# The third channel group of a causal convolution moved from TensorE to GpSimd, ahead of a fused feed-forward

## The chip, the cores and the metric

The kernel runs on one core of a Trainium2 chip. The metric is the device time of one execution in microseconds (us). The engines' names in the profile are PE (TensorE; PEld is its weight load), DVE (VectorE), ACT (ScalarE), POOL (GpSimd) and SP (SyncE, which here only issues DMAs).

## The reference, cut to what matters

```python
batch, seq, d_model = 8, 3904, 192      # x: (8, 3904, 192) float32
n_heads, kernel_size, d_ff = 8, 7, 1024

def _attn_ref(x, weight):               # a causal convolution of 7 taps along seq
    w = softmax(weight, axis=-1)        # (heads, 7); a head is 24 channels
    x_pad = np.concatenate([np.zeros((B, 6, D)), x], axis=1)
    x_unf = x_pad[:, idx, :].reshape(B, S, K, H, group)
    return np.einsum('hk,bskhg->bshg', w, x_unf).reshape(B, S, D)

def _moe_ref(x, w1, w2, w3, w_out):     # over 31232 tokens of 192 channels
    return ((x @ w1) * (x @ w2)) @ w3 @ w_out
```

## The kernel before, in words

The 31232 tokens are held as two strips of 15616 (NS = 2, strip r), which are worked on side by side. The 192 channels are held as three groups of 64; in each of the tiles xT[0], xT[1] and xT[2] the partitions are 64 channels of strip 0 and the same 64 of strip 1, and the columns are tokens. These tiles are rings of 2048 tokens, four rounds of 512 (CH).

The product w3 @ w_out is formed once at the start. Then each of 31 rounds R of 512 tokens has two steps. `first_product(R)` (L385 to L394) multiplies xT[0], xT[1], xT[2] by w1 and w2 in that order of k, accumulating in PSUM; ScalarE copies one result to SBUF (asb, L392), VectorE multiplies it with the other (abT, L394). `second_product(R, r)` (L410, L415, L418) multiplies abT by the joined weights, ScalarE copies the result out (osb), and SP issues the DMA to the output.

The convolution is itself a matmul. Windows of 32 tokens (26 new ones and 6 from before) lie on 32 partitions, loaded by GpSimd's queue with a cast to bf16 (`load_x`, tile xb, L117); a 32x32 band matrix of one head's taps (Aband) gives 26 convolved tokens. TensorE does 16 such small matmuls per head piece (`conv`, L282) into the PSUM tile cps; VectorE and ScalarE cast it into convo (L290). `store` (L315, L321) writes convo to the DRAM tensor rows from SP's queue, 26 rows a window, and `transposes(R)` (L355) brings 512 rows of each of the three groups back as xT, by a transposing DMA on SP's queue.

Windows come in blocks: SIZES gives 11 blocks of 20 to 80 windows. A unit is one call of conv for some heads of a block. From block 4 on there are 26 units.

The order of the steady part is written out by hand. Its phases p = 0 to 14 have the first products of two rounds each (none in phase 0, rounds 2p+1 and 2p+2 after it), then the second products of the two rounds before. Between second products stand convolution units: after the first and the third of four, and in phases 0 and 1 after the second too. The last unit of a block is followed by that block's stores. At a phase's end the transposes of two rounds are issued as far as stored rows allow. Loads of xb for later blocks are issued behind a small copy (pace, L563), with which GpSimd waits for the phase's first round. Where a window begins a sequence, GpSimd sets six rows of xb to zero (L558) once the load has landed.

All engines run their queues in order. A wait on SP holds every later DMA on SP; a wait on GpSimd holds its later loads and copies.

Of the kernel before, what the change touches and what calls it, by code (L numbers as in the profile page):

```python
# [8 lines left out]
FP32 = mybir.dt.float32  # L9
BF16 = mybir.dt.bfloat16  # L10
# [6 lines left out]
def kernel(  # L17
# [10 lines left out]
    nc = tc.nc  # L28
# [26 lines left out]
    MAXN = 20  # L55
    HW = 6

    def tok(i):
# [16 lines left out]
        return stage.tile(shape, dtype, tag="slot", bufs=5, name=name)  # L75

    rows = dram.tile([TS, NP * NS * Q], BF16, name="rows")
    x_rows = x.rearrange("b s d -> (b s) d")


    def shape_of(b):
        n = SIZES[b] // 4
        m = n // (1 if b < 3 else 2)
        return n, m, n // m

    def parts_of(b):
        return [range(4)] if 4 * shape_of(b)[1] <= MAXN else [range(2), range(2, 4)]

    xb_of, zero_rows = {}, {}

# [15 lines left out]
    def load_x(b, parts=(0, 1)):  # L106
        tiles = xb_of.setdefault(b, {})
        zeros_of = zero_rows.setdefault(b, [])
        n, m, E = shape_of(b)
        for js in [v for q, v in enumerate(parts_of(b)) if q in parts]:  # L110
            xb = work.tile([128, len(js) * m, D], BF16, tag="xb", bufs=6, name="xb")
            for j in js:
                tiles[j] = (xb, (j - js[0]) * m)
            for e in range(E):
                for s, t, w in runs_of(b, js, e):
                    for r in range(NS):
                        nc.gpsimd.dma_start(  # L117
                            out=xb[group(r, e), s:s + w, :],
                            in_=bass.AP(tensor=x.tensor, offset=(r * TS + t - PAD) * D,
                                        ap=[[D, C], [E * ST * D, w], [1, D]]))  # L120
                for j in js:
                    for u in range(m):
                        i, s = FIRST[b] + j * n + u * E + e, tiles[j][1] + u
                        if i % WB == 0 and i:
                            zeros_of += [(xb, group(r, e).start, s) for r in range(NS)]
                        if i == NWIN - 1:
                            nc.gpsimd.memset(xb[group(1, e), s, :], 0.0)
                            t = tok(i) - PAD
                            nc.gpsimd.dma_start(out=xb[group(0, e), s, :],
                                                in_=x_rows[t:t + C, :])  # L130
                            p = group(1, e).start
                            nc.gpsimd.dma_start(out=xb[p:p + PAD + LAST, s, :],
                                                in_=x_rows[TS + t:TS + t + PAD + LAST, :])


    taps = const.tile([H, K], FP32)
# [115 lines left out]

    xT = [const.tile([128, RING], BF16, name=f"xT{k}", tag=f"xT{k}") for k in range(NP)]

    convo_of, heads_left = {}, {}
    wt = {}

    def segments(c0, n):
# [4 lines left out]
            c0, n = c0 + m, n - m  # L263
        return out

    def conv(b, h0, nh, evict=(nc.scalar.copy,), es=None):
        n, m, E = shape_of(b)
        es = range(E) if es is None else es
        if b not in convo_of:
            convo_of[b] = work.tile([128, n, NP, NS, Q], BF16, tag="convo", bufs=2, name="convo")  # L270
            heads_left[b] = H * E
        convo = convo_of[b]
        wd = nh * G
        cps = {e: banks("cps") for e in es}
        for q in range(nh):
            cs = slice((h0 + q) * G, (h0 + q + 1) * G)
            for j in range(4):
                xb, s = xb_of[b][j]
                for e in es:
                    for r in range(NS):  # L280
                        o = cps[e][j * C:j * C + C, r, 0:m * wd]
                        nc.tensor.matmul(  # L282
                            o.rearrange("p (w g) -> p w g", g=wd)[:, :, q * G:(q + 1) * G],
                            Aband[group(r, e), h0 + q, :], xb[group(r, e), s:s + m, cs],
                            start=True, stop=True)
        for f, e in zip(evict, es):
            src = cps[e][:, :, 0:m * wd].rearrange("p r (w g) -> p r w g", g=wd)
            o = 0
            for k, c0, c in segments(h0 * G, wd):
                f(out=convo[:, e::E, k, :, c0:c0 + c]  # L290
                    .rearrange("p w r g -> p r w g"), in_=src[:, :, :, o:o + c])
                o += c
        heads_left[b] -= nh * len(es)
        if not heads_left[b]:
            del xb_of[b]

    stored, sent = [0], [3]
# [1 line left out]
    def store(b, first=0):  # L299
        stored[0] = tok(FIRST[b] + SIZES[b]) if b + 1 < NB else TS  # L300
        n = SIZES[b] // 4
        convo = convo_of[b]
        for j in range(4):
            w = 0
            while w < n:
                i = FIRST[b] + j * n + w
                if i < first:
                    w += 1
                    continue
                left = WB - 1 - i % WB  # L310
                src = convo[C * j:C * j + ST, w:w + max(1, min(n - w, left))]
                src = src.rearrange("s w k r g -> s w (k r g)")
                j0 = tok(i)
                if left == 0:
                    nc.sync.dma_start(out=rows[j0:j0 + LAST, :], in_=src[0:LAST, 0, :])  # L315
                    w += 1
                    continue
                m = min(n - w, left)
                dst = rows[j0:j0 + ST * m, :].rearrange("(w s) c -> s w c", s=ST)
                for s0, s1 in ((0, 16), (16, ST)):  # L320
                    nc.sync.dma_start(out=dst[s0:s1], in_=src[s0:s1])  # L321
                w += m
# [28 lines left out]
    def transposes(R, first=0):  # L351
        t0, t1 = max(R * CH, first), min((R + 1) * CH, TS)
        a = t0 % RING
        for k in range(NP):
            nc.sync.dma_start_transpose(  # L355
                out=xT[k][:, a:a + t1 - t0], in_=rows[t0:t1, k * 128:(k + 1) * 128])


    def w_of(i, k, r):
        if k == 2:  # L360
# [119 lines left out]

    conv(0, 0, 4, evict=(A,))
    swap_w(0, 0, 256, P)
    conv(0, 4, 4, evict=(V,))
    warm(2)
    first_transposes()
    for k in (2, 1):
# [29 lines left out]
    first_product(0, {  # L518
        0: seq((swap_w, 1, 256, HC, A, (1,))),
        2: later_loads,  # L520
        4: seq((conv, 1, 0, 4)),
        5: seq((conv, 1, 4, 4)),
        6: seq((pe_transposes, 1))})
    first_product(1, {
        2: seq((conv, 2, 0, 4)),
        3: seq((conv, 2, 4, 4), (w3_turn, 0)),
        4: seq((pe_transposes, 2), (store, 2, LAG_ROWS // ST))})
    first_product(2, {
        1: seq((w3_turn, 2)),
        3: seq((w3_product, 0), (w3_product, 2), (w3_turn, 4), (w3_turn, 6),  # L530
               (conv, 3, 0, 4, (A,), (0,)), (conv, 3, 0, 4, (V,), (1,))),
        4: seq((w3_product, 4), (w3_product, 6),
               (conv, 3, 4, 4, (A,), (0,)), (conv, 3, 4, 4, (V,), (1,)),
               (store, 3), (transposes, 3), (transposes, 4))})
    sent[0] = 5


    phases = [()] + [(R, R + 1) for R in range(LAG + 1, NR, 2)]
    assert phases[-1][-1] == NR - 1
    def heads_of(b):  # L540
        return max(n for n in (2, 4, 8) if n * shape_of(b)[1] * G <= CH)

    units = [(b, h, heads_of(b)) for b in range(4, NB) for h in range(0, H, heads_of(b))]
    loads = [(b, e) for b in range(6, NB) for e in range(len(parts_of(b)))]

    def convolve():
        if units:
            b, h, n = units.pop(0)
            conv(b, h, n, (V, A))
            if h + n == H:  # L550
                store(b)

    pace = const.tile([1, 2], BF16)
    done = 0
    for p, rounds in enumerate(phases):
        for b, h, n in units[:3]:
            for xb, p0, w in zero_rows.pop(b, []):
                nc.gpsimd.memset(xb[p0:p0 + PAD, w, :], 0.0)  # L558
        for j, R in enumerate(rounds):
            first_product(R)  # L560
            if loads and (j == 0 or p == 1):
                nb, part = loads.pop(0)
                P(out=pace, in_=abT_of[R][0:1, JT - 1, 1, 0:2])  # L563
                load_x(nb, (part,))
# [43 lines left out]
```

## Time and profile before

| | |
|---|---|
| median of 3 runs | 519.27 us (518.94 to 520.60) |
| profiled execution | 519.05 us, span 517.2 us |
| granted TensorE clock | 1.0 of full |
| busy: PE, DVE, ACT, POOL | 99%, 66%, 64%, 14% of the span |
| convolution matmuls L282 | 1216, 15.5 us busy |
| DMA | 64.81 MB, mean 125 GB/s |
| xb loads on GpSimd's queue (L117) | 74, 48.0 us busy |

Busy times are sums over instructions; matmuls overlap, and their ends are modelled, so a PE that reads 99% tells that it rarely waits, not that it is at its peak. The chain of waits leads from the last instruction back through what released each step. A timeline gives start, duration, engine, line and count of merged instructions, and in brackets the idle time ahead and who ended it.

### The profile page before, as it was taken

How to read it: one execution, taken by the hardware profiler on the slowest of the kernel's cores; microseconds unless marked ns; L12 is line 12 of the kernel's file. 1: busy time of each engine (PE TensorE's matmuls, PEld its weight loads, DVE VectorE, ACT ScalarE, POOL GpSimd, SP SyncE). 2: the span in 40 equal slices, each digit the busy share in tenths (PEclk: the TensorE clock that was granted, in tenths of full speed). 3: DMA queues.
4: the chain of work that ended last, by engine and by line, in shares of the span. 5: the costliest groups of instructions: out<-in, count | busy, mean ns of one | idle time of the engine just before them, and what ended most of it. 6: DMA issues, size and time to landing. Idle time of an engine off the chain costs nothing.

```text
span 517.2 us, 14447 instructions
## 1 busy us (share of the span) xinstructions
PE 511.6 (99%) x6271; PEld 333.4 (64%) x6272; DVE 343.5 (66%) x326; ACT 332.6 (64%) x376; POOL 73.3 (14%) x140
## 2 busy tenths in 40 slices
PE   8999999999999999999999999999999999999997
PEld 4446946758567585674856758567585575856777
DVE  7898478494783947839578395783946839377370
ACT  6886476674765757657576575765757657476562
POOL 9864004030020200402002020030000000000000
PEclk9999999999999999999999999999999999999999
DMA  9999779999666995669956696456725066240304
GB/s 146 150 185 176 143 187 158 223 120 186 118 77 151 149 152 119 77 142 155 151 123 77 147 166 120 123 61 143 146 84 123 1 147 137 64 107 2 123 1 153
DMA packets 137936, 64.81 MB, mean 125 GB/s; under 512 B 86805, under 2 KB 137873, under 8 KB 137873
## 3 DMA queue, kind: packets, MB, share of 16 engines
q1 hardware_dynamic: 92625, 45.92, 42.1%
q0 software_dynamic: 45232, 17.97, 31.5%
q8 instruction: 49, 0.80, 0.6%
q14 instruction: 14, 0.11, 0.1%
q10 hardware_dynamic: 16, 0.00, 0.0%
HBM read 36.22 MB, written 34.80 MB: 137 GB/s over the span
## 4 chain that ended last, share of the span: by engine, by line
PE 97%; DVE 1%; ACT 1%; issue 0%; DVEq 0%
PE ops L410 32%; PE pa L385 30%; PE pb L385 30%; PE cps L282 2%; PE wps L475 1%; PE warm L196 1%; ACT asb L392 1%; DVE abT L394 0%; ACT convo L290 0%; PE ops L428 0%; PE tps L345 0%; PE tps L330 0%; DVE xT L337 0%; DVE xb L238 0%; DVE Aband L248 0%
## 5 line engine op out<-in xcount | busy, mean ns | idle before, releaser
L394 DVE TENSOR_TENSOR abT<-asb,pb 128x1024 bf16<-128x1024 bf16 x240 | 292.7, 1220 | 81.5 <-ACT asb L392 65.7
L392 ACT CAST asb<-pa 128x1024 bf16<-128x1024 f32 x244 | 247.0, 1012 | 63.4 <-PE pa L385 63.1
L385 PE MATMUL pb<-xT,wn 64*128 64x512 bf16 (+1 forms) x744 | 198.4, 373 | 0.0
L385 PE MATMUL pa<-xT,wn 64*128 64x512 bf16 (+1 forms) x744 | 197.5, 373 | 0.2
L385 PE MATMUL pa<-xT,ws 64*128 64x512 bf16 (+1 forms) x744 | 197.5, 373 | 0.0
L385 PE MATMUL pb<-xT,ws 64*128 64x512 bf16 (+1 forms) x744 | 196.1, 373 | 0.0
L385 PEld LDWEIGHTS <-wn 64*128 64x128 bf16 x1488 | 138.1, 94 | 85.7 <-issue 2.2
L385 PEld LDWEIGHTS <-ws 64*128 64x128 bf16 x1488 | 131.5, 94 | 70.8 <-POOL ws L182 0.4
L410 PE MATMUL ops<-W_sb,abT 128*128 128x192 bf16 x1936 | 166.9, 246 | 0.0
L410 PEld LDWEIGHTS <-abT 128*128 128x128 bf16 x1936 | 157.6, 98 | 10.0 <-issue 9.4
L415 ACT COPY osb<-ops 128x768 f32<-128x768 f32 (+1 forms) x61 | 48.4, 793 | 108.8 <-PE ops L410 106.5
L290 DVE CAST convo<-cps 128x320 bf16<-128x320 f32 (+5 forms) x46 | 33.8, 766 | 75.4 <-PE cps L282 73.8
L117 POOL DMA_DIRECT2D xb<-in_x_dram x74 | 48.0, 656 | 7.3 <-PE pa L385 3.2
L563 POOL COPY pace<-abT 1x2 bf16<-1x2 bf16 x10 | 1.7, 174 | 245.1 <-DVE abT L394 245.1
L290 ACT CAST convo<-cps 128x640 bf16<-128x640 f32 (+5 forms) x54 | 32.5, 645 | 1.7 <-PE cps L282 1.6
L282 PE MATMUL cps<-xb,Aband 32*32 32x240 bf16 (+2 forms) x1216 | 15.5, 245 | 0.5 <-DVE Aband L248 0.4
L282 PEld LDWEIGHTS <-Aband 32*32 32x32 bf16 x1216 | 8.4, 88 | 7.1 <-issue 6.3
L432 DVE COPY osb<-ops 128x192 f32<-128x192 f32 x1 | 0.4, 357 | 11.7 <-PE ops L428 11.7
L456 POOL DMA_DIRECT2D w3b<-in_moe_w_dram x12 | 7.1, 598 | 4.0 <-DMA xb<-in_x_dram 3.1
L182 POOL COPY ws<-wn 64x256 bf16<-64x256 bf16 x17 | 6.7, 396 | 0.9
L196 PE MATMUL warm<-zeros 128*128 128x512 bf16 (+1 forms) x12 | 4.6, 518 | 1.4 <-DVE zeros L140 1.3
L475 PEld LDWEIGHTS <-w3T 128*128 128x128 bf16 x64 | 5.2, 98 | 1.0 <-issue 0.4
(57 smaller groups left out, 54.1 us busy)
## 6 DMA issues: line engine op xcount, KB each, us to landing
out_dram<-osb SPq DMA_DIRECT2D x60, 384.0 KB
xb<-in_x_dram POOLq DMA_DIRECT2D x40, 240.0 KB, 7.0
rows<-convo SPq DMA_DIRECT2D x17, 240.0 KB
rows<-convo SPq DMA_DIRECT2D x17, 150.0 KB
xb<-in_x_dram POOLq DMA_DIRECT2D x8, 192.0 KB, 4.4
rows<-convo SPq DMA_DIRECT2D x12, 120.0 KB
xT<-rows SPq DMA_TRANSPOSE x84
w3b<-in_moe_w_dram POOLq DMA_DIRECT2D x4, 256.0 KB, 5.0
```

What stands on the lines that cost most here:

```text
L117: nc.gpsimd.dma_start(out=xb[group(r, e), s:s + w, :], in_=bass.AP(tensor=x.tensor, offset=(r * TS + t - PAD) * D, ap=[[D, C], [E * ST * D ...
L182: f(out=wsw[k][Q * h:Q * h + Q, lo:hi], in_=wn[k][Q - Q * h:2 * Q - Q * h, lo:hi])
L196: nc.tensor.matmul(t[:, j % 2, 0:wd], zeros[:, 0:128], zeros[:, 0:wd], start=True, stop=True)
L282: nc.tensor.matmul(o.rearrange("p (w g) -> p w g", g=wd)[:, :, q * G:(q + 1) * G], Aband[group(r, e), h0 + q, :], xb[group(r, e), s:s + m, ...
L290: f(out=convo[:, e::E, k, :, c0:c0 + c] .rearrange("p w r g -> p r w g"), in_=src[:, :, :, o:o + c])
L385: nc.tensor.matmul(p[:, r, f * N:f * N + N], w_of(i, k, r)[rs, ft * 128:(ft + 1) * 128], xT[k][rs, r0:r0 + N], start=(k == 0), stop=(k == ...
L392: nc.scalar.copy(out=asb[:, :, 0:per * N], in_=pa[:, :, 0:per * N])
L394: nc.vector.tensor_tensor(out=ab[:, f0, :, 0:N], in0=asb[:, :, 0:N], in1=pb[:, :, 0:N], op=ALU.mult)
L410: nc.tensor.matmul(ops[:, g // 2, (g % 2) * D:(g % 2) * D + D], ab[:, jt, r, g * 128:(g + 1) * 128], W_sb[:, jt, :], start=(jt == 0), stop ...
L415: nc.scalar.copy(out=osb.rearrange("p (a g) d -> p a (g d)", g=2), in_=ops[:, 0:ng // 2, 0:2 * D])
L456: nc.gpsimd.dma_start(out=t[C * i:C * i + C], in_=bass.AP(tensor=moe_w3.tensor, offset=j0 * 128 * DFF + i * GQ, ap=[[DFF, C], [C * DFF, 4 ...
L475: nc.tensor.matmul(wps[:, q, 0:D], w3T[:, g, q, :, :, t].rearrange("p j b -> p (j b)"), wo_b[:, g, t, :], start=(g + t == 0), stop=(g == G ...
```

## The change

Three things change from block 4 (round 5) on.

TensorE convolves only channels 0 to 127. Blocks 4 to 11 have 64 windows (the last 56), and a unit is 64 channels of a block, so that there are 16 units; since heads are 24 channels wide, a unit has three or four pieces of heads. A table (places) says how many units a phase has. xb, convo, rows stores and the transposes of xT cover 128 channels.

Channels 128 to 191 go another way. A DMA on GpSimd's queue casts them from x to a DRAM tensor rows_c in bf16 (`cast_c`), 1024 tokens of both strips at a time (a chunk; 13 chunks). A transposing DMA on SP's queue, issued at the end of phase p after the last output and before the transposes of xT, brings chunk p as the tile raw, with 16 tokens from before it (`raw_transpose`). In phase p+1 GpSimd convolves it: for each tap a multiply of raw, shifted by the tap's distance, with a column of taps, and an add to acc, in float32; the tap of distance 0 comes last, in two halves, and writes xT[2] (`conv_c`). Where a sequence starts inside a chunk, each step is split in two. The products of phase p+2 read it.

The taps reach GpSimd as a tile wC, one row per partition, through a small DRAM tensor: GpSimd divides by the sum, and SP issues seven small DMAs (`load_taps`) before the stores of blocks 2 and 3.

On GpSimd's queue the order of a phase is: zero rows, the cast of chunk p, the convolution of chunk p-1, pace, loads of xb.

```diff
-    SIZES = [20, 20, 20, 40, 40] + [80] * 5 + [64]
+    SIZES = [20, 20, 20, 40] + [64] * 7 + [56]
+    SPLIT = 4
+    WC = 2 * Q
...
+    RC = FIRST[SPLIT] * ST // CH
...
+    def width_of(b):
+        return D if b < SPLIT else WC
...
-            xb = work.tile([128, len(js) * m, D], BF16, tag="xb", bufs=6, name="xb")
+            wd = width_of(b)
+            xb = work.tile([128, XN], BF16, tag="xb", bufs=6, name="xb")
+            xb = xb[:, 0:len(js) * m * wd].rearrange("p (w d) -> p w d", d=wd)
...
-    def conv(b, h0, nh, evict=(nc.scalar.copy,), es=None):
+    def conv(b, c0, wd, evict=(nc.scalar.copy,), es=None):
...
-        for q in range(nh):
-            cs = slice((h0 + q) * G, (h0 + q + 1) * G)
+        c = c0
+        while c < c0 + wd:
+            h = c // G
+            c1 = min(h * G + G, c0 + wd)
             for j in range(4):
...
-                            Aband[group(r, e), h0 + q, :], xb[group(r, e), s:s + m, cs],
+                            Aband[group(r, e), h, :], xb[group(r, e), s:s + m, c:c1],
...
-        for k in range(NP):
+        for k in range(NP if R < RC else WC // Q):
             nc.sync.dma_start_transpose(
                 out=xT[k][:, a:a + t1 - t0], in_=rows[t0:t1, k * 128:(k + 1) * 128])
...
+    def load_taps():
+        nc.sync.dma_start(out=taps_d, in_=taps)
+        for r in range(NS):
...
+                nc.sync.dma_start(out=wC[r * Q + c - WC:r * Q + c1 - WC, :],
+                                  in_=taps_d[h:h + 1, :].to_broadcast([c1 - c, K]))
...
+    def cast_c(i):
+        t0, t1 = chunks[i]
+        t0 = t0 if i else t0 - HALO
+        for r in range(NS):
+            nc.gpsimd.dma_start(out=rows_c[t0:t1, r * Q:r * Q + Q],
+                                in_=x_rows[r * TS + t0:r * TS + t1, WC:D])
+
+    def raw_transpose(i):
+        t0, t1 = chunks[i]
+        raw_of[i] = work.tile([128, HALO + 2 * CH], BF16, tag="raw", bufs=2, name="raw")
+        nc.sync.dma_start_transpose(out=raw_of[i][:, 0:HALO + t1 - t0],
+                                    in_=rows_c[t0 - HALO:t1, :])
+
+    def conv_c(i):
+        t0, t1 = chunks[i]
+        raw = raw_of.pop(i)
+        acc = work.tile([128, 2 * CH], FP32, tag="acc", bufs=1, name="acc")
+        part = work.tile([128, 2 * CH], FP32, tag="part", bufs=1, name="part")
+        starts = [z for z in range(0, TS, S) if t0 <= z < t1]
+
+        def times(out, lo, hi, d):
+            nc.gpsimd.tensor_scalar(out=out, in0=raw[:, HALO + lo - t0 - d:HALO + hi - t0 - d],
+                scalar1=wC[:, K - 1 - d:K - d], scalar2=None, op0=ALU.mult)
+
+        def add(out, lo, hi, d):
+            p = part[:, lo - t0:hi - t0]
+            times(p, lo, hi, d)
+            nc.gpsimd.tensor_tensor(out=out, in0=p, in1=acc[:, lo - t0:hi - t0], op=ALU.add)
+
+        times(acc[:, 0:t1 - t0], t0, t1, 1)
+        for z in starts:
+            nc.gpsimd.memset(acc[:, z - t0:z - t0 + 1], 0.0)
+        for d in range(2, K):
+            for lo, hi in zip([t0] + [z + d for z in starts], starts + [t1]):
+                add(acc[:, lo - t0:hi - t0], lo, hi, d)
+        for lo in range(t0, t1, CH):
+            hi = min(lo + CH, t1)
+            add(xT[2][:, lo % RING:lo % RING + hi - lo], lo, hi, 0)
...
-        for b in (4, 5):
-            load_x(b)
+        load_x(4)
+        nc.gpsimd.tensor_scalar(out=taps, in0=taps, scalar1=total, scalar2=None, op0=ALU.mult)
+        load_taps()
+        cast_c(0)
+        load_x(5)
...
-    units = [(b, h, heads_of(b)) for b in range(4, NB) for h in range(0, H, heads_of(b))]
+    units = [(b, c) for b in range(SPLIT, NB) for c in range(0, WC, Q)]
...
+    places = {0: 2, 1: 2, 2: 1, 3: 1, 4: 2, 5: 1, 6: 1, 7: 1, 8: 1, 9: 2, 10: 1, 11: 1}
...
+        if 0 < p < len(chunks):
+            cast_c(p)
+        if 0 < p <= len(chunks):
+            conv_c(p - 1)
         for j, R in enumerate(rounds):
             first_product(R)
-            if loads and (j == 0 or p == 1):
+            if loads and j == 0:
...
-            if n in (0, 2) or (n == 1 and p < 2):
+            if n in (0, 2)[:places.get(p, 0)]:
                 convolve()
+        if p < len(chunks):
+            raw_transpose(p)
```

More of the change, by code (lines that the diff above doesn't have):

```diff
@@ L288, in conv @@
             o = 0
[L289 to L290 removed]
+            for k, lo, c in segments(c0, wd):
+                f(out=convo[:, e::E, k, :, lo:lo + c]
                     .rearrange("p w r g -> p r w g"), in_=src[:, :, :, o:o + c])
                 o += c
[L293 to L294 removed]
+        left_of[b] -= wd * len(es)
+        if not left_of[b]:
             del xb_of[b]
@@ new lines @@
+    chunks = [(R * CH, min((R + 2) * CH, TS)) for R in range(RC, NR, 2)]
+    raw_of = {}
+    def cast_c(i):
[9 more added lines that the diff above has]
+                                    in_=rows_c[t0 - HALO:t1, :])
```

65 lines of the change are left out of this document (37 added, 28 removed).

## The prediction, made before the changed kernel was run

> **What bounds the kernel now.** I read the page first (busy times, chain), then the stretches of single phases, then the groups by shape, then the timelines of SyncE and GpSimd, because the new work is handed over through those two queues.
>
> ```profile
> PE 511.6 (99%) x6271; PEld 333.4 (64%) x6272; DVE 343.5 (66%) x326; ACT 332.6 (64%) x376; POOL 73.3 (14%) x140
> PE 97%; DVE 1%; ACT 1%; issue 0%; DVEq 0%
> ```
>
> TensorE carries 97% of the chain that ended last, while VectorE and ScalarE have a third of the span free. So only two things move the end: TensorE work removed, and TensorE waits added. The profiled execution took 519.05 us (span 517.2 us, 1.85 us around it); the median of the runs is 519.27 us, 0.04% away. I sum against 519.05. A measurement of this kernel can tell about 0.3%, 1.6 us, from no change.
>
> Four phases (two rounds of products each), as stretches: length, then busy time and instructions of PE, PEld, DVE, ACT, POOL, clock, DMA share, GB/s.
>
> ```profile
> 65.00:97.86 32.86, 32.86 (x418) 21.06 (x420) 23.13 (x21) 22.06 (x25) 5.70 (x10) 1.00 1.19 183
> 195.10:227.52 32.42, 32.42 (x387) 21.02 (x388) 21.91 (x19) 21.13 (x23) 5.50 (x11) 1.00 0.56 105
> 357.19:389.52 32.33, 32.33 (x386) 20.94 (x388) 21.51 (x19) 20.81 (x23) 0.00 (x0) 1.00 0.58 124
> 421.86:453.35 31.49, 31.49 (x322) 20.67 (x324) 19.53 (x16) 19.34 (x20) 0.00 (x0) 1.00 0.50 113
> ```
>
> They hold three, two, two (192 columns) and no convolution units. The differences are the whole price of convolution on TensorE: 32.42 - 31.49 = 0.93 us for two units of 32 matmuls of 240 columns, 0.84 us for two of 192 columns.
>
> Groups by shape:
>
> ```profile
> L282 PE MATMUL cps<-xb,Aband 32*32 32x240 bf16 x640 | 8.5, 266 | 0.0
> L282 PE MATMUL cps<-xb,Aband 32*32 32x120 bf16 x448 | 5.5, 216 | 0.5 <-DVE Aband L248 0.4
> L394 DVE TENSOR_TENSOR abT<-asb,pb 128x1024 bf16<-128x1024 bf16 x240 | 292.7, 1220 | 81.5 <-ACT asb L392 65.7
> L182 POOL COPY ws<-wn 64x256 bf16<-64x256 bf16 x17 | 6.7, 396 | 0.9
> L563 POOL COPY pace<-abT 1x2 bf16<-1x2 bf16 x10 | 1.7, 174 | 245.1 <-DVE abT L394 245.1
> ```
>
> **TensorE: what is removed.** From block 4 on, the kernel before issues 896 convolution matmuls (128 in block 4, 640 in blocks 5 to 9, 128 in block 10). The changed kernel has 8 blocks of 7 head pieces x 16 = 112, again 896: the cuts at channels 64 and 128 split heads, so a third fewer channels gives no fewer instructions (its instruction order shows as many PE rows as before). And the price goes by instruction, hardly by column: the chain shows 64 matmuls of 120 columns in 0.66 us (10.3 ns each), 32 of 240 in 0.35 (10.9). What falls is the 0.1 us that each unit costs in switching: 26 units become 16. Before, phase 0 pays 12.64 us for four output products that take 10.67 in a phase without units, so 1.97; phase 1 pays 1.37; eight phases 0.93; two 0.84: 12.5 us in all. After: a pair of units has 48 + 64 matmuls, 112 x 10.1 ns + 2 x 0.1 = 1.33, eight pairs 10.7. Saving **1.8 us**; bounds 1.0 (nothing per matmul, ten switches) and 4 (a third of the 12.5).
>
> ScalarE and VectorE lose a third of the evictions at L290 and DMA a third of the stores and xb bytes. Worth nothing here: they lie under TensorE, and if that cover went they would save under 1 us a phase.
>
> **GpSimd: what is added.** Per chunk of 1024 tokens: a multiply (d=1), five times multiply and add (d=2..6), and d=0 as two halves of 512. No row shows these forms on GpSimd. The nearest: a copy of 256 elements takes 396 ns and one of 2 elements 174, so 0.17 us fixed and 0.87 ns an element net, 1.55 gross. Low bound: an add costs what a copy does (1.06 us for 1024, chunk 15 us). High bound: gross rate, an add reading two operands in turn (3.2 us, chunk 34 us). I take 1.0 ns an element and operand, near the net rate because the instructions are long, a little above it because sums are float32: multiply 0.17 + 1.02 = 1.2, add 0.17 + 2.05 = 2.2. Chunk: 1.2 + 5 x 3.4 + 2 x (0.68 + 1.19) = 22.0; each instruction waits for the one before it, 0.07 us by diag's memset and select (1.03 to 1.10), x15 = 1.0. **23 us**, first half of xT[2] ready after 21. Three chunks that hold a sequence start split every step: +2.5.
>
> The Trainium skill's "GPSIMD Engine Reference", section 3, has 4497 ns for a float32 add of 2048; an estimate from it is 2.25 us for 1024, beside the 2.2 above. The same section keeps elementwise work on VectorE, which speaks against this change; by its add price with the copy rows for multiplies the chunk is 22 us.
>
> A phase is 32 us, so GpSimd's sum (23, casts 1.6, loads 2.7 to 5.4) fits. What must be asked is when a chunk may start and must end. The raw of phase p is convolved in phase p+1 for the products of phase p+2. It must end (first half) by the start of the next phase's products plus 0.45 us, as TensorE can do the k=0 and k=1 matmuls first. It may start when the raw transpose landed, and that stands on SP behind the out DMAs and, in some phases, the stores:
>
> ```profile
> 66.65 1.13 SPq L418 DMA_DIRECT2D out_dram<-osb  x2
> 67.89 6.06 SPq L321 DMA_DIRECT2D rows<-convo  x8
> ...
> 187.12 9.21 SPq L418 DMA_DIRECT2D out_dram<-osb  x4
> 196.43 8.04 SPq L355 DMA_TRANSPOSE xT<-rows  x6
> 219.54 6.11 SPq L418 DMA_DIRECT2D out_dram<-osb  x3
> 226.11 0.76 SPq L321 DMA_DIRECT2D rows<-convo  x2
> 226.96 0.25 SPq L315 DMA_DIRECT2D rows<-convo  x1
> 227.27 9.57 SPq L321 DMA_DIRECT2D rows<-convo  x8
> 236.94 1.42 SPq L418 DMA_DIRECT2D out_dram<-osb  x1
> 238.46 12.12 SPq L355 DMA_TRANSPOSE xT<-rows  x6
> ```
>
> Phases end at 195.10 and 227.52. Without stores SP reaches its transposes 1.3 us after the end; behind stores of an 80-window block 10.9 us after it. A 64-window block has 0.8 of that, so about 8. A transpose of 512 rows takes 1.2 us to issue, 1040 rows 2.4; landing is not shown, I take 2 (0 to 5). So raw lands at end + 5.7 in plain phases, + 8.4 where stores come in mid-phase (3, 6, 8, 11), + 12.4 where they come last (1, 4, 9). Phase 0: SP starts its outs at 66.65; three outs 1.7, stores of 64 windows 6.06 x 1.6 = 9.7, one out, transpose 2.4, landing: 82.
>
> - Chunk 0: 82 + 21.1 = 103.1; TensorE needs it at 97.85 + 0.45. **Wait 4.8 us.**
> - Plain phases: 5.7 + 21.1 = 26.8 of about 32.2: hidden, 5 us to spare. Mid-phase stores: 29.5, hidden.
> - Late stores (phases 4 and 9): 12.4 + 21.1 = 33.5 against 32.7: **0.8 us each**.
> - Phase 3: chunk 1 (a split one, raw late) ends late, then eight loads of 0.67, then the memset of zero rows waits for that load to land (5 us), and the cast and chunk 2 stand behind it on GpSimd. Carried through phase by phase: **2.6 us** at the start of phase 4.
>
> Sum of waits 9.0. **519.05 - 1.8 + 9.0 = 526.3 us.**
>
> ```profile
> 207.36 0.17 POOL L563 COPY pace<-abT 1x2 bf16<-1x2 bf16 x1 [29.19 <-DVE abT L394]
> 207.90 4.83 POOL L117 DMA_DIRECT2D xb<-in_x_dram  x8 [0.36 <-PE pa L385]
> ```
>
> These loads now come after the chunk, some 15 to 25 us later. They fill blocks used one or two phases on, and land in 7 us: I cost that at nothing; with the cover gone a load would cost the first unit up to 10 us, once. The tap loads stand on SP before the stores of block 3, which wait for their eviction until 49 us anyway: nothing, at most 1 us.
>
> VectorE's product L394 has one operand in PSUM and one in SBUF. The Trainium skill's "SBUF — State Buffer", section on the shared port rule, has GpSimd blocked only by VectorE instructions with two SBUF inputs or in a two-port mode; by that no contention, and no run here shows it.
>
> **Rivals.**
> 1. GpSimd hides everything (faster). If a chunk takes at most 17.5 us (an add at 1.4 us), even chunk 0 is ready in time: 519.05 - 1.8 = **517.2 us**. For it: 17.5 lies inside my bounds, and one-operand copies run at 0.87 ns. Against: an add reads two operands and float32.
> 2. Between 17.5 and 21 us only chunk 0 waits, by 0 to 3 us: **517.5 to 520**, no difference.
> 3. GpSimd becomes the bound. From 27 us on, late raws, loads and casts add up and most phases wait: at 1.2 ns an operand the same reckoning gives 31 us of waits, **548 us**; at the gross rate (34 us) some 91, **608 us**. For it: the gross rate is the only one that a row shows without subtraction.
> 4. The saving is absent: if units cost by matmul and the switch is not saved, 1.8 us are missing from each case. Within the ranges.
>
> After a wait TensorE may restart slowly: at the start, six warm matmuls of 512 columns take 2.74 us, about twice their later rate. The Trainium skill's "TensorE: Matmul & The Clock Gate", Part 1, has half clock after an idle window of about 3.4 us; one such restart would add an estimated 2 us, inside the range.
>
> **Numbers.** Forecast case (chunk 21 to 27 us, 520.6 to 545) 0.44; rival 1 0.18; rival 2 0.11; rival 3 0.27. Faster 0.18, same 0.11, slower 0.71. The range from 517 (rival 1) to 549 (rival 3's first price) leaves out about 0.2, nearly all above.
>
> **What would show it.** Right: POOL groups near 1.2 (multiply) and 2.2 us (add); the longest TensorE gap, near 5 us, before the round-5 products at about 98 us, released by POOL's add into xT; smaller ones at the starts of phases 4, 6, 11; phases without waits 0.2 us shorter than before. Wrong: no PE wait on POOL (rival 1), waits at every phase (rival 3), PE phases shorter by over 0.4 us (convolution priced by column), waits on xb loads or on rows transposes, or L394 longer than 1220 ns (port contention).

## The result and the profile after

The changed kernel takes 625.93 us (median of 4 runs, 625.21 to 626.58), the kernel before beside it 519.11 us: ratio 1.2044, interval 1.2022 to 1.2066, 106.8 us slower. The forecast was 526.3 us, with 549 at the end of its range.

The page of the changed kernel (profiled execution 626.58 us, span 624.9 us): busy times, the granted TensorE clock in 40 slices, and the chain that ended last, by engine and by line.

```profile
PE 532.8 (85%) x6271; PEld 350.4 (56%) x6272; DVE 333.0 (53%) x302; ACT 325.0 (52%) x352; POOL 529.1 (85%) x371
PEclk9999997699897997996998979999799898999999
POOL 74%; PE 18%; DMA 3%; issue 3%; ACT 0%; DVE 0%; POOLq 0%; SPq 0%; DVEq 0%
```

GpSimd was busy 14% and is busy 85%, and the chain has passed from TensorE (97% before) to GpSimd (74%). TensorE's busy time rose by 21 us with as many matmuls as before, and its clock is no longer full in every slice.

The groups by shape on GpSimd and VectorE (form and count, busy us and mean ns, idle time ahead and its releasers):

```profile
L411 POOL TENSOR_SCALAR part<-raw,wC 128x1024 f32<-128x1024 bf16 x45 | 128.0, 2844 | 3.5
L417 POOL TENSOR_TENSOR acc<-part,acc 128x1024 f32<-128x1024 f32 x45 | 105.7, 2349 | 3.7
L411 POOL TENSOR_SCALAR part<-raw,wC 128x512 f32<-128x512 bf16 x25 | 39.1, 1565 | 1.2
L417 POOL TENSOR_TENSOR xT<-part,acc 128x512 bf16<-128x512 f32 x25 | 31.6, 1265 | 2.1
L464 DVE TENSOR_TENSOR abT<-asb,pb 128x1024 bf16<-128x1024 bf16 x240 | 292.9, 1221 | 232.7 <-PE pb L455 151.3 <-ACT asb L462 67.2
```

The add took 2.35 us (forecast 2.2). The multiply, which has only one tensor to read, took 2.85 us (forecast 1.2): it is the slower of the two. VectorE's product abT takes 1221 ns (1220 before).

The waits (engine, line and what it waited for: us in total, times, longest), then lines of the timelines of SP, TensorE and GpSimd:

```profile
PE pa L455 <- POOL xT L417: 86.2, 12, 18.0
POOL acc L411 <- DMA raw<-rows_c: 36.3, 2, 34.7
```

```profile
77.57 1.89 SPq L400 DMA_TRANSPOSE raw<-rows_c  x1
83.52 2.85 POOL L411 TENSOR_SCALAR acc<-raw,wC 128x1024 f32<-128x1024 bf16 x1 [34.68 <-DMA raw<-rows_c]
...
116.17 0.58 PE L455 MATMUL pa<-xT,wn 64*128 64x512 bf16 x1 [17.98 <-POOL xT L417]
...
118.96 0.18 POOL L638 COPY pace<-abT 1x2 bf16<-1x2 bf16 x1
119.08 3.17 POOL L127 DMA_DIRECT2D xb<-in_x_dram  x4
122.24 1.53 POOL L394 DMA_DIRECT2D rows_c<-in_x_dram  x2
123.81 2.86 POOL L411 TENSOR_SCALAR acc<-raw,wC 128x1024 f32<-128x1024 bf16 x1
```

All twelve phases from 2 to 13 wait for GpSimd, 86.2 us in all. GpSimd itself waits for raw in earnest only once, before chunk 0; from then on it goes from chunk to loads to cast to the next chunk. Chunk 0 takes from 83.52 to 118.96, 35.4 us, and the next begins 40.3 us after it began, while a phase of TensorE needs 32. From chunk 0 to chunk 11, which begins at 526.99, the mean period is 40.3 us.

Where the time went, by the first matmuls of phases 2 and 14, in the kernel before and then in the changed one:

```profile
97.79 0.39 PE L385 MATMUL pa<-xT,wn 64*128 64x512 bf16 x1
484.77 0.39 PE L385 MATMUL pa<-xT,wn 64*128 64x512 bf16 x1
...
97.59 0.39 PE L455 MATMUL pa<-xT,wn 64*128 64x512 bf16 x1
592.41 0.39 PE L455 MATMUL pa<-xT,wn 64*128 64x512 bf16 x1
```

Phase 14 begins 107.6 us later, and that is the whole difference of the spans (624.9 less 517.2). Between the two starts, TensorE's phases take 107.8 us longer: 86.2 us of waits, and 21.6 us net of slower matmuls after them and of the smaller convolution.

### The profile page after: what moved, and what is told of

It is laid out like the page before. It is cut to its first block, busy times and chain, and to the rows that moved or that the text cites. A ratio compares the mean times of both kernels' runs of the same rounds, so it can differ in the third digit from the quotient of the medians.

```text
span 624.9 us, 14657 instructions
## 1 busy us (share of the span) xinstructions
PE 532.8 (85%) x6271; PEld 350.4 (56%) x6272; DVE 333.0 (53%) x302; ACT 325.0 (52%) x352; POOL 529.1 (85%) x371
## 4 chain that ended last, share of the span: by engine, by line
POOL 74%; PE 18%; DMA 3%; issue 3%; ACT 0%; DVE 0%; POOLq 0%; SPq 0%; DVEq 0%
POOL part L411 34%; POOL acc L417 23%; PE pa L455 6%; POOL acc L411 5%; PE pb L455 5%; PE ops L480 5%; POOL xT L417 4%; POOL xb L127 4%; POOL rows_c L394 2%; DMA raw<-rows_c 2%; POOL ws L192 1%; PE wps L545 1%; DMA wn<-in_moe_w_dram 1%; DMA xb<-in_x_dram 1%; PE cps L294 0%
## 5 line engine op out<-in xcount | busy, mean ns | idle before, releaser
L464 DVE TENSOR_TENSOR abT<-asb,pb 128x1024 bf16<-128x1024 bf16 x240 | 292.9, 1221 | 232.7 <-PE pb L455 151.3
L455 PE MATMUL pa<-xT,wn 64*128 64x512 bf16 (+1 forms) x744 | 210.2, 389 | 86.4 <-POOL xT L417 86.2
L411 POOL TENSOR_SCALAR part<-raw,wC 128x1024 f32<-128x1024 bf16 (+9 forms) x106 | 226.1, 2133 | 5.1
L455 PE MATMUL pb<-xT,wn 64*128 64x512 bf16 (+1 forms) x744 | 212.0, 389 | 0.0
L455 PE MATMUL pa<-xT,ws 64*128 64x512 bf16 (+1 forms) x744 | 210.3, 389 | 0.0
L417 POOL TENSOR_TENSOR acc<-part,acc 128x1024 f32<-128x1024 f32 (+8 forms) x80 | 152.7, 1908 | 6.7
L411 POOL TENSOR_SCALAR acc<-raw,wC 128x1024 f32<-128x1024 bf16 (+1 forms) x13 | 36.4, 2802 | 36.8 <-DMA raw<-rows_c 36.3
L303 DVE CAST convo<-cps 128x1024 bf16<-128x1024 f32 (+3 forms) x22 | 23.0, 1055 | 42.4 <-PE cps L294 42.4
L417 POOL TENSOR_TENSOR xT<-part,acc 128x512 bf16<-128x512 f32 (+1 forms) x26 | 32.4, 1244 | 2.2
L303 ACT CAST convo<-cps 128x1024 bf16<-128x1024 f32 (+3 forms) x30 | 23.2, 800 | 1.9 <-PE cps L294 1.8
L394 POOL DMA_DIRECT2D rows_c<-in_x_dram x26 | 20.2, 779 | 1.5 <-issue 1.4
L294 PE MATMUL cps<-xb,Aband 32*32 32x192 bf16 (+6 forms) x1216 | 14.4, 225 | 0.6 <-DVE Aband L258 0.5
```

What stands on the lines that cost most here:

```text
L294: nc.tensor.matmul(o.rearrange("p (w g) -> p w g", g=wd)[:, :, c - c0:c1 - c0], Aband[group(r, e), h, :], xb[group(r, e), s:s + m, c:c1], ...
L303: f(out=convo[:, e::E, k, :, lo:lo + c] .rearrange("p w r g -> p r w g"), in_=src[:, :, :, o:o + c])
L394: nc.gpsimd.dma_start(out=rows_c[t0:t1, r * Q:r * Q + Q], in_=x_rows[r * TS + t0:r * TS + t1, WC:D])
L411: nc.gpsimd.tensor_scalar(out=out, in0=raw[:, HALO + lo - t0 - d:HALO + hi - t0 - d], scalar1=wC[:, K - 1 - d:K - d], scalar2=None, op0=AL ...
L417: nc.gpsimd.tensor_tensor(out=out, in0=p, in1=acc[:, lo - t0:hi - t0], op=ALU.add)
L455: nc.tensor.matmul(p[:, r, f * N:f * N + N], w_of(i, k, r)[rs, ft * 128:(ft + 1) * 128], xT[k][rs, r0:r0 + N], start=(k == 0), stop=(k == ...
```

## The experiments

The theory: GpSimd's chunk is the bound, because its multiply has a price of its own, so the time follows the chunk. Rivals: the late raw, the restarts of TensorE's clock, or a contention with VectorE make the loss.

**e1, the price of the disputed operation by itself.** The kernel before, with GpSimd instructions on unused memory put into phases 3 to 12 behind the pace copy; nothing reads their results.

```diff
+            g.tensor_scalar(out=sf[2], in0=sb[0], scalar1=sw, scalar2=None, op0=ALU.mult)
+            g.tensor_scalar(out=sf[2], in0=sb[0], scalar1=0.5, scalar2=None, op0=ALU.mult)
+            g.tensor_scalar(out=sf[2], in0=sf[0], scalar1=sw, scalar2=None, op0=ALU.mult)
...
+            g.tensor_copy(out=sf[2], in_=sb[0])
...
+            g.tensor_tensor(out=sf[2], in0=sf[0], in1=sf[1], op=ALU.add)
...
+            g.tensor_tensor(out=sf[2], in0=sb[0], in1=sf[1], op=ALU.mult)
```

> The kernel before, with GpSimd instructions on scratch tiles of 128x1024 added in phases 3 to 12, behind the loads; nobody reads their results. It puts a row beside each price that the prediction had to bound. Multiply by a scalar: if reading the scalar from a tile is what made it 2.85 us instead of 1.2, the form with a constant in the instruction takes 1.1 to 1.3; if it is the bf16 input, the form with a float32 input takes 1.1 to 1.3; if the multiply itself has its rate on GpSimd, all four forms take 2.5 to 2.9. Copies: 1.06 by the early copies of 256 elements. Adds: 2.35 for two float32 inputs; with bf16 inputs 2.35 too if elements are counted, 1.2 to 1.8 if bytes are. The whole: 519.1 if GpSimd beside TensorE costs nothing, and L394 stays at 1220 ns; if VectorE and GpSimd take turns at a port, L394 is longer and the time above 525.

Measured: 519.40 us, ratio 1.0003 (0.9993 to 1.0012), and VectorE's abT stays at 1221 ns. Its groups by shape:

```profile
L570 POOL TENSOR_SCALAR w3b<-w3b,sw 128x1024 f32<-128x1024 bf16 x4 | 11.4, 2852 | 0.3
L571 POOL TENSOR_SCALAR w3b<-w3b 128x1024 f32<-128x1024 bf16 x4 | 11.1, 2769 | 0.3
L572 POOL TENSOR_SCALAR w3b<-w3b,sw 128x1024 f32<-128x1024 f32 x4 | 11.4, 2838 | 0.4
L575 POOL CAST w3b<-w3b 128x1024 f32<-128x1024 bf16 x3 | 3.2, 1054 | 0.0
L578 POOL TENSOR_TENSOR w3b<-w3b 128x1024 f32<-128x1024 f32 x3 | 7.0, 2345 | 0.0
L583 POOL TENSOR_TENSOR w3b<-w3b 128x1024 f32<-128x1024 bf16 x3 | 6.4, 2137 | 0.0
```

A multiply by a scalar takes 2.8 us whether the scalar is a column in memory or a constant, and whatever the input's type. A cast of the same tile takes 1.05. A product of two whole tensors (L583) takes 2.14: less than the product with one number for each partition. Adds with bf16 inputs take 2.13 to 2.14, which neither of the two expectations for them had. So neither the number of operands nor a subtracted fixed cost gives the price; the operation has its own. The kernel of 519 us bears such work without a loss as long as nobody waits for it.

**e2, the whole new path with a short chunk.** Only the taps of distance 0, 1 and 2 are taken; the four others are left out.

```diff
-        for d in range(2, K):
+        for d in range(2, 3):
```

> The changed kernel with only the taps of distance 0, 1 and 2 in the GpSimd convolution (the other four are left out); all casts, raw transposes, tap loads and hand-overs stay. A chunk is then 2.85 + 5.3 + 2 x 2.94 = 14 us instead of 35.4. If the chunk's length is the whole loss, no TensorE wait on xT[2] is left (first chunk 83.5 + 11.2 = 94.7, needed at 97.6), and the time is that of before less the saving on TensorE: 517.3 (516.5 to 518). If the rest of the new path (casts, raw transposes, SP's queue, DMA traffic) costs time by itself, it is above 519.

Measured: 517.91 us, ratio 0.9965 (0.9952 to 0.9979). Waits of GpSimd:

```profile
POOL acc L411 <- DMA raw<-rows_c: 192.1, 12, 35.0
```

Now GpSimd waits for raw in every phase, and TensorE nowhere for xT[2]. Casts, transposes, loads and the moved queues cost nothing that can be seen. What TensorE gains can be read from the starts of its phases: phase 0 takes 12.05 us (12.65 before), a phase with one unit 32.14 to 32.21 (32.33 to 32.42, with two), but phases 4 and 9, with units of 48 and 64 matmuls where there were two of 32, take 32.88 (32.42). Summed over the phases, 1.4 us.

**e3, raw earlier.** The transpose of raw(0) goes ahead of the transposes of rounds 3 and 4, the later ones behind the first output of a phase instead of its last.

```diff
-               (store, 3), (transposes, 3), (transposes, 4))})
+               (store, 3), (raw_transpose, 0), (transposes, 3), (transposes, 4))})
...
+            if n == 0 and 0 < p < len(chunks):
+                raw_transpose(p)
```

> The changed kernel with each raw transpose issued earlier on SP: that of chunk 0 after the stores of block 3, the others after a phase's first output instead of its last. If one unbroken chain on GpSimd sets the end, the time falls by as much as chunk 0 starts earlier (83.5 to about 63 us, 20) and by the one later wait for raw (about 5): 600 to 606, and the period from chunk to chunk stays at 37 to 43 us. If hand-overs in every phase set the period, it falls by several us in each of 12 phases: below 580. If neither is on the path: 626.

Measured: 602.47 us, ratio 1.1595 (1.1557 to 1.1633). Chunks begin at 59.99, 100.31, 147.24 and 187.53 us, where they began at 83.52, 123.81, 170.53 and 210.83: the same chain, 23.5 us earlier, and 23.5 us come off the time. The period did not move. So raw's time sets where the chain begins, once; it is not what makes each phase long.

**e4, TensorE kept busy in its waits.** Matmuls on zeros, whose results are not read, fill most of each wait.

```diff
+    idle = {2: 70, 3: 38, 4: 46, 5: 28, 6: 38, 7: 38, 8: 38, 9: 10, 10: 38, 11: 14, 12: 14, 13: 14}
...
+            if j == 0 and p in idle:
+                warm(idle[p])
```

> The changed kernel with matmuls on zeros (10 to 70 of 512 columns, 216 ns each at full clock) put ahead of each phase's products from phase 2 to 13, as many as fill the wait for xT[2] but for 3 us. They keep TensorE busy, so that it does not restart at half clock. If the chain on GpSimd sets the end, TensorE's slow restarts lie under it: 622 to 626, only the last one, 2 us, on the path. If the half clock is part of the loss (PE's busy time rose by 21 us), about 605.

Measured: 625.21 us, ratio 1.2022 (1.1998 to 1.2046), as without it. Its waits, and its clock:

```profile
PE pa L455 <- POOL xT L417: 15.3, 8, 2.8
```

The mean granted clock rose from 0.929 to 0.989, and chunks begin at 83.42, 123.72 and 170.40 us, as they did. The slow matmuls lie beside GpSimd's chain, not on it: they cost nothing as long as GpSimd is the bound. Only the last restart, in phase 13, has no later wait for GpSimd behind it: in the changed kernel that phase lasts 36.94 us, 1.9 more than the 31.49 of a phase without units and its wait of 3.59. In e4 its first matmul after the wait is slow too, so this part is not tested.

**e5, the multiply alone exchanged.** The product is taken as one of two tensors, the second being the tap's column repeated.

```diff
-            nc.gpsimd.tensor_scalar(out=out, in0=raw[:, HALO + lo - t0 - d:HALO + hi - t0 - d],
-                scalar1=wC[:, K - 1 - d:K - d], scalar2=None, op0=ALU.mult)
+            nc.gpsimd.tensor_tensor(out=out, in0=raw[:, HALO + lo - t0 - d:HALO + hi - t0 - d],
+                in1=wC[:, K - 1 - d:K - d].to_broadcast([128, hi - lo]), op=ALU.mult)
```

> The changed kernel with one edit: each multiply by a scalar on GpSimd is written as a product of two tensors, the second being the tap's column repeated along the tokens. By the price rows such a product takes 2.13 us for 1024 instead of 2.85. If the chunk on GpSimd sets the end, a chunk falls from 35.4 by 7 x 0.72 = 5 us to 30.4, the twelve periods fall with it until TensorE's phase of 32.2 us is reached in those without loads, and the time is 570 to 582. If the repeated column is read no faster than a scalar, 626; if something else paces the phases, above 600.

Measured: 569.22 us, ratio 1.0972 (1.0954 to 1.0991). Its group by shape and its wait:

```profile
L411 POOL TENSOR_TENSOR part<-raw,wC 128x1024 f32<-128x1024 bf16 x45 | 85.2, 1893 | 2.8
```

```profile
PE pa L455 <- POOL xT L417: 39.7, 8, 12.4
```

One instruction's form is worth 57 us. The repeated column is read even faster than a whole second tensor (1.89 against 2.14 us). Chunk 0 takes 28.6 us (83.79 to 112.35), four of twelve phases no longer wait, and the time lies a little under what was expected as the product was priced at 2.13.

**e6, the products on VectorE, the adds on GpSimd.** VectorE multiplies in bf16 in the pauses of its own work, between second products; the cast and raw come a phase earlier for it; xb has five buffers in place of six, to make room.

```diff
+            nc.vector.tensor_scalar(out=o, in0=raw[:, HALO - d:HALO + t1 - t0 - d],
                 scalar1=wC[:, K - 1 - d:K - d], scalar2=None, op0=ALU.mult)
...
+        nc.gpsimd.tensor_tensor(out=acc[:, 0:n], in0=prods[:, 1, 0:n], in1=prods[:, 2, 0:n],
+                                op=ALU.add)
...
+    spread_c = ((1, 2), (3, 4), (5, 6), (0,))
...
+                multiply_c(p, spread_c[n] if p else (range(K) if n == 3 else ()))
```

> The new path with its parts where the rows put them: VectorE multiplies (bf16 products of 1024 tokens, two behind each second product, in a part of the phase where it is idle about 9 of 11 us), GpSimd only adds (5 of 2.1 and 2 of 1.2 us, 13.5 a chunk), the cast is issued a phase earlier, the raw transpose at a phase's start, that of chunk 0 before the transposes of round 3; xb has 5 buffers. If the multiply on GpSimd and the late raw were all that was wrong, no TensorE wait on xT[2] is left and the time is that of the run with three taps, 517.3 to 518.2, 0.3% under the kernel before. If VectorE's products delay its evictions or the loads, TensorE waits on them and the time is above 519.

Measured: 543.36 us, ratio 1.0466 (1.0445 to 1.0488). GpSimd no longer holds TensorE, but VectorE does, in twelve waits for abT:

```profile
PE pb L460 <- DVE abT L469: 20.0, 12, 5.2
```

VectorE's product of raw and a tap takes 1440 ns in the mean. e7, e8 and e9 ask why.

**e7, products split between VectorE and ScalarE.** As e6, with taps 2, 4 and 6 on ScalarE, and raw(0) ahead of block 3's stores. The order of the products is also changed, so that GpSimd's first add needs the last one.

```diff
-    spread_c = ((1, 2), (3, 4), (5, 6), (0,))
+    spread_c = ((0, 2), (3, 4), (5, 6), (1,))
...
+            if d in on_act:
+                nc.scalar.activation(out=o, in_=src, func=ACT.Copy, scale=tap)
```

> The version with VectorE's products, changed in three places: three of the seven products of a chunk (distances 2, 4, 6) go to ScalarE, about 1.0 us each by its casts, between its output copies; GpSimd's first add needs the product that VectorE makes last, so that adds and products no longer run at the same time; the raw transpose of chunk 0 is issued before the stores of block 3. VectorE then has 4 x 1.2 and ScalarE 3 x 1.0 us more in the 11 us of second products, where they are idle about 9 and 6. If seven products of 1.2 to 2.2 us on VectorE were what held up its abT products (33.8 us a phase), the phases fall back to 32.2 us and the time to 517.3 to 518.5. If products beside GpSimd's adds or ScalarE's later copies still hold up PSUM, it is 520 to 535.

Measured: 525.23 us, ratio 1.011 (1.0093 to 1.0127). The products on VectorE and on ScalarE:

```profile
L416 DVE TENSOR_SCALAR prods<-raw,wC 128x1024 bf16<-128x1024 bf16 x48 | 21.0, 480 | 20.6 <-issue 10.4 <-DMA raw<-rows_c 7.6 <-DMA rows<-convo 2.7
L414 ACT ACTIVATE prods<-raw,wC 128x1024 bf16<-128x1024 bf16 x36 | 41.6, 1155 | 10.3 <-DMA raw<-rows_c 7.6 <-DMA rows<-convo 2.7
```

VectorE's product takes 480 ns now, ScalarE's 1155, and the phases from 2 on take 32.2 us, as in e2. What is lost lies in phases 0 and 1, where the stores come later behind raw(0) and raw(1) lands late (VectorE and ScalarE wait 7.6 us each for it); TensorE's clock is at half there too (0.50 from 67.7 to 71.0 us and from 101.9 to 108.5). More than one thing was changed against e6, so this run does not tell which of them made the product fast.

**e8 and e9, one thing apart.** All products on VectorE in both. In e8 the first add needs the last product; in e9 the first two, so that the adds begin beside the products. The diff goes from e8 to e9:

```diff
-    spread_c = ((0, 2), (3, 4), (5, 6), (1,))
+    spread_c = ((1, 2), (3, 4), (5, 6), (0,))
```

> VectorE makes all seven products, ScalarE none; GpSimd's first add needs the product that VectorE makes last, so that its adds start when the products are done; the raw transpose of the next chunk is issued at a phase's end ahead of the transposes of xT, that of chunk 0 behind the stores of block 3. If a VectorE product takes 0.48 us when no GpSimd add runs, as in the run before, seven are 3.4 us, well within its idle time in the second products, no wait is left and the time is 517.3 to 518.3, that of the run with three taps. If something besides the products (five xb buffers, late loads, the raw transpose ahead of the xT transposes) holds up TensorE, it is above 519.

> The same but for the order of the products: GpSimd's first add needs the two that VectorE makes first, so adds and products run at the same time. If GpSimd's adds shut VectorE's products out of a shared port while they run, a product takes 1.2 to 2.2 us again, seven 8 to 10 us, abT is late and the time is 530 to 545. If the slow products of that earlier run came from something else (the raw transpose, the cast), it is as fast as the run with the adds after the products.

Measured: e8 519.37 us, ratio 1.0016 (1.0 to 1.0031); e9 541.67 us, ratio 1.0434 (1.0418 to 1.0451). The group of the products in e8, then in e9:

```profile
L412 DVE TENSOR_SCALAR prods<-raw,wC 128x1024 bf16<-128x1024 bf16 x84 | 35.7, 482 | 0.8 <-DMA xT<-rows 0.2
```

```profile
L412 DVE TENSOR_SCALAR prods<-raw,wC 128x1024 bf16<-128x1024 bf16 x84 | 116.7, 1440 | 0.8
```

And the timeline of one such place, VectorE and GpSimd, in e8 and then, with TensorE, in e9:

```profile
157.74 2.86 DVE L412 TENSOR_SCALAR prods<-raw,wC 128x1024 bf16<-128x1024 bf16 x7
160.75 2.11 POOL L423 TENSOR_TENSOR acc<-prods 128x1024 f32<-128x1024 bf16 x1 [11.46 <-DVE prods L412]
...
164.59 10.39 DVE L412 TENSOR_SCALAR prods<-raw,wC 128x1024 bf16<-128x1024 bf16 x7
165.61 2.23 POOL L423 TENSOR_TENSOR acc<-prods 128x1024 f32<-128x1024 bf16 x1 [9.47 <-DVE prods L412]
167.93 9.05 POOL L426 TENSOR_TENSOR acc<-prods,acc 128x1024 f32<-128x1024 bf16 x4
...
176.16 0.37 PE L460 MATMUL pb<-xT,wn 64*128 64x512 bf16 x1 [1.42 <-DVE abT L469]
```

Seven products that take 2.86 us in e8 take 10.39 here, until GpSimd's adds are nearly through, and then TensorE waits for the abT that stood behind them. The same instruction is three times as long while GpSimd adds, and GpSimd's adds to acc are hardly slower (2.20 us for 2.14). The Trainium skill's "SBUF — State Buffer", section "Who interferes with whom", says that VectorE's tensor-by-scalar operations can take the port pair that it shares with GpSimd, and that whoever comes first holds it for a whole instruction; e8 and e9 agree (482 against 1440 ns). They show the slowing; that this port pair is its cause is the page's account, which no run here sets apart from another.

**e10 and e11, the start of e8.** e8's phases from 2 on are as in e2 (for one, 132.27 to 164.48 us: 32.2), yet its time is that of the kernel before. Its profile shows 1 us lost before phase 0 and one gap of 1.2 us in a convolution unit. e10 moves two things, e11 only the second.

```diff
-               (store, 3), (raw_transpose, 0), (transposes, 3), (transposes, 4))})
+               (store, 3), (transposes, 3), (transposes, 4), (raw_transpose, 0))})
...
+        load_x(5)
         cast_c(0)
         cast_c(1)
-        load_x(5)
```

> The kernel of e8 with two things moved at its start: the transposing DMA of raw(0) goes behind the transposes of rounds 3 and 4 (in e8 it stands ahead of them), and the loads of block 5's windows go ahead of the first two casts (in e8 behind them). In e8 phase 0's outputs start at 53.8 us, in e2 at 52.9 us; one gap of 1.2 us inside a convolution unit at 96 us has no releaser that the trace shows. Theory 'order at the start': what GpSimd and VectorE do is hidden, the new path gains 1.8 us on TensorE, and e8 loses it to where its DMAs stand at the start; then phase 0 starts near 53 us and the time is 517.5 to 518.3 us, 0.2 to 0.3% under before. Rival 'the third group has a price of its own': the gain is spent beside VectorE's products (their 0.5 us each in VectorE's queue ahead of an abT), whatever the order; then the steady phases are not shorter than in e8 and the time stays at 519.2 to 519.6 us.

Measured: 526.30 us, ratio 1.0133 (1.0116 to 1.015). Both expectations missed. The timeline:

```profile
71.95 2.87 DVE L412 TENSOR_SCALAR prods<-raw,wC 128x1024 bf16<-128x1024 bf16 x7 [7.70 <-DMA raw<-rows_c]
...
76.00 0.58 PE L460 MATMUL pa<-xT,wn 64*128 64x512 bf16 x1 [6.37 <-DVE abT L469]
```

VectorE's products of chunk 0 stand in its queue ahead of round 3's abT; with raw(0) late, abT waits behind them and TensorE behind abT. The phase's first products take 22.4 us beside the wait, where 20.8 is usual: the restart at a lower clock (0.76 of full from 76 to 82 us) costs 1.6 us here, where no other engine covers it.

> The kernel of e8 with one thing moved: the loads of block 5's windows go ahead of the first two casts on GpSimd's queue; raw(0) stays ahead of the transposes of rounds 3 and 4, as in e8. In e10 raw(0) behind them landed 7.7 us too late for VectorE's products of chunk 0, which stand in VectorE's queue ahead of round 3's abT, and TensorE waited 6.4 us; apart from that wait e10's phases were as in e2, without the 1.2 us gap of e8 at 97 us. Theory 'order at the start': that gap came with the casts ahead of the loads; without it the time is 517.6 to 518.6 us. Rival 'a price of the new path': the gap or another like it stays, and the time is 519.0 to 519.6 us.

Measured: 519.87 us, ratio 1.0006 (0.9993 to 1.0018). The gap is there again:

```profile
97.56 0.21 PE L294 MATMUL cps<-xb,Aband 32*32 32x64 bf16 x4 [1.44 <-issue]
```

So the loads' place did not make it: the expectation that the gap stays was right, and the time lies 0.3 us above the end it gave. The gap stands in e7, e8 and e11 ahead of the last four of 64 matmuls of a unit in phase 1 (2.35, 1.24 and 1.44 us), not in e2 or e10, and has no releaser in the trace. One record bears on it: in these three runs a packet of the queue that loads instructions (q8) starts 2.4 to 2.5 us before TensorE goes on (at 98.3, 94.8 and 95.1 us), while in e2 one starts at 89.8, well ahead of that place. A late load of TensorE's own instructions would fit this, but the trace does not tell for which engine a load is. What it waits for stays open, and so does a version that beats the kernel before: e8 and e11 equal it.

## Why the prediction was wrong

**The step that failed: "multiply 0.17 + 1.02 = 1.2".** It took a net rate from copies and carried it over to a multiply by a scalar. Measured, it is 2.85 us. Six of 1024 were priced 9.9 us too low, two of 512 (1.57 for 0.68) another 1.8: 11.7 of the 12.4 us by which chunk 0 passed the 23 forecast. The adds, 2.35 and 1.27 for 2.2 and 1.19, make the rest; the gaps between instructions were right (0.97 us in chunk 0 for 1.0). e1 shows the price by itself, and e5 that this instruction alone is worth 57 us. The Trainium skill's "GPSIMD Engine Reference", section 4.1, calls one-input work on GpSimd roughly line-rate; that holds here for copies (1.05 us), not for the multiply by a scalar. The same section sends elementwise work to VectorE, and e8 and e9 bear that out for the product (0.48 us on VectorE alone).

**What that turned over.** Each wait in the sum was worked out from the 23 us. The first half of xT[2] was to be ready 21.1 us into chunk 0 and was after 32.6, and the chunk began at 83.5 for 82: the first wait, 4.8, becomes 4.8 + 11.5 + 1.5 = 17.8, and 17.98 was measured. The others were to be 0.8 to 2.6 at three phases; instead a chunk with loads and cast, 40 us, passed the phase's 32, and every phase waits. That is rival 3, whose mechanism was right: it gave 608 us at a chunk of 34, and twelve chunks longer by 1.4 us make 625. That its 34 lay so near the measured 35.4 is in part luck. At the gross rate of 1.55 ns, which already holds the fixed cost, the chunk adds up to 31; 34 comes out only if the 0.17 us of each instruction are added a second time. And the rate had the multiply too short (1.6 us for 2.85) and the add too long (3.2 for 2.35). What was wrong there was its weight, 0.27, and a range that ended at its first price (549) though its second, the gross rate, was, as the text says, the only one that a row showed without subtraction. The rate taken, 1.0 ns, lay near the low bound, at which no multiply or add had been seen.

**What held.**
- TensorE's saving: 1.8 us forecast, 1.4 us by e2's phases, 1.8 us by its ratio (1.1 to 2.5). A pair of units costs 1.38 us for the 1.33 forecast. That phases 4 and 9 become longer by 0.45 was not said.
- Raw(0) behind outs and stores on SP: the forecast had it land at 82; it was issued at 77.57, and GpSimd began at 83.52. The terms that the forecast names add up to 83.0, not 82, and two errors in them cancel: the stores took 8.3 us of SP for 9.7, while the transpose took 1.89 to issue for 2.4 and about 4 to land for 2.
- Later raws, loads, casts and tap loads hidden: e2 shows TensorE without a wait on any of them.
- Rival 1's condition, a chunk of at most 17.5 us: in e2, with a chunk of 14.0 us, no phase waits.
- No contention for abT, 1220 ns before and 1221 after, as the prediction had it from its one operand in PSUM. e9 shows the other side of the rule, with a VectorE operation that reads and writes SBUF only.
- Half clock after a wait: seen, but off the path in the changed kernel (e4) up to the last restart, which cost 1.9 us; 1.6 us where it was on the path in e10. The estimate was 2.

## What to carry to other kernels

A rate belongs to an operation, not to an engine: a copy's time says nothing of a multiply's on the same engine, and where no row shows the form, the slowest row of that engine belongs inside the range. When work is moved to an idle engine, compare its whole period there (work, loads, casts, gaps) with the period of the bound engine first, since past that point each further microsecond counts once per stage. And where GpSimd shares work with VectorE, try their SBUF-to-SBUF instructions one after the other, not side by side: VectorE's products and GpSimd's adds, the one pair tried here, gave 519 us in turn and 542 us together.

## What the runs showed of the hardware

GpSimd multiplies a tile of 1024 by a scalar in 2.85 us, but by a repeated column, as a second tensor, in 1.89, and casts it in 1.05. VectorE does the bf16 product by a scalar in 0.48 us, and ScalarE in 1.16.

TensorE's clock can fall after work has begun again. After waits of 4.9 us and more (e3, the changed kernel) the first matmul is already slow; of two waits of 3.9 us, it is slow after that of e3 (0.58 us) and not after that of e9 (0.37). After 4.24 us (e5) the first is at full speed, and matmuls of 0.63 us come 0.9 us later. After 1.78 us none is slow. The length of the wait does not decide it alone: in e4, where matmuls on zeros fill most of the wait, 2.07 us without a matmul were enough (clock 0.50 from 158.6 to 162.0 us), and 2.78 us were not (1.00 from 116.1 to 119.0). After 3.59 us, in the changed kernel, the first matmul runs at full speed and matmuls at half speed come 1.3 us later:

```profile
559.66 0.37 PE L455 MATMUL pa<-xT,wn 64*128 64x512 bf16 x1 [3.59 <-POOL xT L417]
...
560.97 0.62 PE L455 MATMUL pa<-xT,ws 64*128 64x512 bf16 x1
561.36 0.63 PE L455 MATMUL pb<-xT,wn 64*128 64x512 bf16 x1
...
564.38 0.38 PE L455 MATMUL pb<-xT,wn 64*128 64x512 bf16 x1
```

From about 560.9 to 564.3 us matmuls take 0.63 us in place of 0.38, and so after the waits of 3.00 and 3.22 us. Three stretches around the wait of 3.00, which ended at 522.7 (length, busy time and count of PE, PEld, DVE, ACT, POOL, then the granted clock, DMA share, GB/s):

```profile
522.70:523.30 0.60, 0.58 (x6) 0.34 (x7) 0.00 (x0) 0.15 (x1) 0.60 (x1) 1.00 1.00 274
523.40:526.80 3.40, 3.40 (x20) 1.44 (x18) 1.39 (x2) 1.77 (x2) 3.32 (x4) 0.50 0.78 172
527.00:530.00 3.00, 3.00 (x30) 1.61 (x28) 2.31 (x3) 2.02 (x2) 3.00 (x2) 1.00 1.60 152
```

Full, half for 3.4 us, full again. The Trainium skill's "TensorE: Matmul & The Clock Gate", Part 1, has a free-running window of about 3.4 us by which the clock is set; that the slow stretch is 3.4 us long and does not begin with the work agrees with it.
